# Attention score steps over two key tiles of one query chunk, with 64-row products for the queries' low parts

## The chip, the cores and the metric

One Trainium2 chip, one of its cores. The metric is device time in microseconds (us) of one launch; a kernel's time is the median of its runs. The engines are named as the profile names them: PE (TensorE matmuls), PEld (TensorE weight loads), DVE (VectorE), ACT (ScalarE), POOL (GpSimd), SP (SyncE, from whose queue all DMAs of this kernel are issued).

## The reference, cut to what matters

A squared-ReLU attention without softmax, gated by `u`, followed by a normalized gated feed-forward layer. All inputs are float32; 4 batches of 3008 tokens, width 256, query/key width 64, feed-forward width 1536.

```python
scores = scale * np.matmul(z, z.transpose(0, 2, 1))       # z: [4, 3008, 64], queries and keys are both z
attn = np.maximum(scores, 0.0) ** 2
out = np.matmul(attn, v)                                  # v: [4, 3008, 256]
x = (u * out).reshape(B * S, D)

rms = np.sqrt(np.mean(x * x, axis=-1, keepdims=True) + 1e-06)
xn = x / rms * rms_g
g = xn @ w_gate                                           # [256, 1536]
silu = g * (1.0 / (1.0 + np.exp(-g)))
val = xn @ w_val
y = silu * val @ w_out                                    # [1536, 256]
```

## The kernel before

**Precision.** Products run in a rounded float32 format (`F32R`). A float32 operand is split into a high part (a rounded copy) and a low part (what the copy left out), and a product of two operands becomes several matmuls that add up in one PSUM bank.

**Queries, keys.** `z` lies in memory twice, transposed: 128 rows, the 64 features and the same 64 again. For a chunk `c` of 512 keys, `prep_stat` makes the stationary tile `zst`: `one` (L278, on ACT) writes the high part of all 128 rows, `two` (L282, on DVE) overwrites rows 64 to 127 with the low part. So a key tile of 128 columns holds high parts above and low parts below. For the queries `prep_mov` makes `mh` and `ml`, high and low parts, each in both halves of the rows. A score tile (128 keys x 512 queries) is two matmuls into one `ps` bank: `zst` with `mh` (L366, 128 rows: high x high plus low x high) and `zst` with `ml` (L367, 128 rows: high x low plus low x low).

**Passes.** Work goes in 12 attention passes `phase_a(p)`, p = 0 to 11, three to a batch. A pass takes two neighbouring query chunks (`k` = 0, 1) and goes over the 24 key tiles of the batch in the order `order(p)`; step `i` takes key tile `i` for both chunks. In a step, `emit_s` makes the scores two steps ahead (`s_product` on PE, `s_relu` on ACT, `s_mult` on DVE: relu(s) times s), `emit_l` splits the squared scores one step ahead into `H` (a cast on ACT, L403) and `L` (a subtraction on DVE, L406; L410 for the last key tile), and `emit_av` multiplies them with the values: six matmuls for each chunk (L445, L446, L450) into four accumulators `po`. Four `ps` banks, six `r`, five `H` and five `L` buffers go round.

**Turned tiles.** Scores are symmetric, so some tiles are not computed twice: when a tile is first made, its squared scores go to memory (`halves`, a copy of 128x1024 16-bit words by ACT, L423, or DVE, L421, then a DMA to `kept`), and a later pass reads them back through a transposing DMA (`load_turned`, L345, one DMA for two key tiles of one chunk, into the ring `T` of six buffers). Of 576 score tiles in all, 392 are computed: 48, 48 and 44 in passes 0 to 2, then 44, 28 and 12 in each further batch. In passes 5, 8 and 11 most tiles are turned. Their loads are put at slot `i - 7` of the pass, for both chunks at even `i`.

**Feed-forward passes.** A feed-forward pass (`phase_m`, `Unit`, L644 to L676) for the pair of chunks three passes back follows each attention pass from pass 2 on. A list `pend` of closures carries the last value products of a pass, and `emit_gate` (L475, DVE: accumulator times `u`, then a DMA to `xg`), into what follows. `load_x` (L482) brings `xg` back as `ux`; `norm_jobs` squares, sums and scales it (L504 on ACT first). For p = 1, 4, 7, 10 these jobs run within attention pass p + 1: `load_x` is put at slot 9 there, the squares at slot 11.

**Order.** The order on each engine is the order of the code (a manual schedule). `at(phase, slot, fn)` puts a job into a slot, `hook` runs the slot's jobs in the order in which they were put there. Every engine, and SP's queue, runs its instructions in order, each waiting for what it needs.

Of the kernel before, what the change touches and what calls it, by code (L numbers as in the profile page):

```python
# [8 lines left out]
F32 = mybir.dt.float32  # L9
# [5 lines left out]
ALU = mybir.AluOpType  # L15
# [4 lines left out]
P = 128  # L20
CH = 512
# [9 lines left out]
def kernel(  # L31
# [13 lines left out]
    nc = tc.nc  # L45
    D, NT = uT.shape
    S = NT // batch
    DQK = zT2.shape[0] // 2
# [3 lines left out]
    NK = -(-S // P)  # L52
# [25 lines left out]
    def f32(ap):  # L78
        return ap.bitcast(F32)

    def where(p):

        b, j = divmod(p, NP)
        return b, 2 * j, b * S + j * PAIR, min(PAIR, S - j * PAIR)

    def width(c):
        return min(CH, S - c * CH)
# [10 lines left out]
    def at(phase, slot, fn):  # L98
        jobs[phase, slot].append(fn)
# [125 lines left out]
    zst = {}  # L225
    mov = {}
# [36 lines left out]
    def prep_stat(b, c, shared=None):  # L263
        t0 = c * CH
        n = width(c)
        m = n + TAIL if n < CH else n
        lo = slice(DQK, P)
        tiles = shared if shared is not None else {}

        def load():  # L270
            raw = tiles["raw"] = new_raw("batch" if b else "start")
            nc.sync.dma_start(out=raw[:, :n], in_=zT2[:, b * S + t0:b * S + t0 + n])
            if n < m:
                nc.sync.dma_start(out=raw[:, n:m], in_=zT2[:, (b + 1) * S - TAIL:(b + 1) * S])

        def one():
            z = zst[b, c] = keep.tile([P, CH], F32R, tag=f"zst{c}", name=f"zst{c}")
            nc.scalar.copy(z[:, :m], tiles["raw"][:, :m])  # L278

        def two():  # L280
            raw, z = tiles["raw"], zst[b, c]
            nc.vector.tensor_tensor(z[lo, :m], raw[lo, :m], f32(z[lo, :m]), op=ALU.subtract)  # L282

        return load, one, two

# [33 lines left out]
    att = {}  # L319
# [3 lines left out]
    def order(p):  # L323
        b, c0 = where(p)[:2]
        if p == 0:
            return list(range(NK))
        first = list(range(4 * (c0 + 1), min(4 * (c0 + 2), NK)))
        last = list(range(4 * c0, 4 * c0 + 4))
        return first + [k for k in range(NK) if k not in first and k not in last] + last
# [4 lines left out]
    def is_turned(p, i, k):  # L334
        b, c0 = where(p)[:2]
        kc = order(p)[i] // 4
        return kc < c0 + k and keeps(b, kc, c0 + k)
# [13 lines left out]

    scores = {}

    def s_product(p, i):
        b, c0 = where(p)[:2]
        kt = order(p)[i]
        for k in range(2):
            if is_turned(p, i, k):
                att[p, i, k] = turned.pop((p, i, k))
                continue  # L360
            n = width(c0 + k)
            mh, ml = mov[p, k]
            z = zst[b, kt // 4]
            ks = slice((kt % 4) * P, (kt % 4 + 1) * P)
            ps = ps_s.tile([P, CH], F32, tag="ps", name="ps")
            nc.tensor.matmul(ps[:, :n], z[:, ks], mh[:, :n], start=True, stop=False)  # L366
            nc.tensor.matmul(ps[:, :n], z[:, ks], ml[:, :n], start=False, stop=True)  # L367
            scores[p, i, k] = (n, ps)

    def s_relu(p, i, k):  # L370
        if (p, i, k) in scores:
            n, ps = scores[p, i, k]
            a = att[p, i, k] = work.tile([P, CH], F32, tag="r", name="r", bufs=6)
            nc.scalar.activation(a[:, :n], ps[:, :n], AF.Relu)  # L374

    def s_mult(p, i, k):
        if (p, i, k) in scores:
            n, ps = scores.pop((p, i, k))
            if not is_square(p, i, k):
                a = att[p, i, k]  # L380
                nc.vector.tensor_tensor(a[:, :n], ps[:, :n], a[:, :n], op=ALU.mult)  # L381

    def emit_s(p, i):
        s_product(p, i)
        for k in range(2):
            s_relu(p, i, k)
            s_mult(p, i, k)

    copies = [0]

    def emit_l(p, i, ks=(0, 1)):
        b, c0 = where(p)[:2]
        kt = order(p)[i]
        for k in ks:
            c = c0 + k
            n = width(c)
            a = att[p, i, k]
            hi = moving.tile([P, CH], F32R, tag="H", name="H", bufs=5)
            if is_square(p, i, k):
                nc.scalar.activation(hi[:, :n], a[:, :n], AF.Square)  # L400
                nc.scalar.activation(a[:, :n], a[:, :n], AF.Square)
            else:
                nc.scalar.copy(hi[:, :n], a[:, :n])  # L403
            if kt < NK - 1:
                lo = moving.tile([P, CH], F32R, tag="L", name="L", bufs=5)
                nc.vector.tensor_tensor(lo[:, :n], a[:, :n], f32(hi[:, :n]), op=ALU.subtract)  # L406
            else:
                lo = None
                h = slice(TAIL, P)
                nc.vector.tensor_tensor(hi[h, :n], a[h, :n], f32(hi[h, :n]), op=ALU.subtract)  # L410
            att[p, i, k] = (hi, lo)
            kc = kt // 4
            if kc > c and keeps(b, c, kc):
                if (b, kc, c) not in kept:
                    kept[b, kc, c] = dram.tile([2 * CH, CH], U16, tag=f"kept{kc}{c}", name=f"kept{kc}{c}")
                m = P if kt < NK - 1 else TAIL
                halves = work.tile([P, 2, CH], U16, tag="out", name="halves", bufs=3)
                split = a[:m].bitcast(U16).rearrange("p (q h) -> p h q", h=2)
                copies[0] += 1
                if c0 == 0 and copies[0] % 5 in (1, 3):  # L420
                    nc.vector.tensor_copy(halves[:m], split)  # L421
                else:
                    nc.scalar.copy(halves[:m], split)  # L423
                r0 = 2 * (kt % 4) * P
                nc.sync.dma_start(
                    out=kept[b, kc, c][r0:r0 + 2 * m, :].rearrange("(p h) q -> p h q", h=2), in_=halves[:m]
                )

    acc = {}

    def emit_av(p, i, k):
        b, c0 = where(p)[:2]
        n = width(c0 + k)
        kt = order(p)[i]
        if i == 0:
            for d in range(ND):
                acc[k, d] = ps_a.tile([P, CH], F32, tag=f"acc{k}{d}", name="po")
        po = [acc[k, d] for d in range(ND)]
        hi, lo = att.pop((p, i, k))
        wh, wl = vh[b, kt // 2], vl[b, kt // 2]  # L440
        j = kt % 2
        ends = i == NK - 1
        for d in range(ND):
            ds = slice(d * P, (d + 1) * P)
            nc.tensor.matmul(po[d][:, :n], wh[:, j, ds], hi[:, :n], start=(i == 0), stop=False)  # L445
            nc.tensor.matmul(po[d][:, :n], wl[:, j, ds], hi[:, :n], start=False, stop=(ends and lo is None))  # L446
        if lo is not None:
            for d in range(ND):
                ds = slice(d * P, (d + 1) * P)
                nc.tensor.matmul(po[d][:, :n], wh[:, j, ds], lo[:, :n], start=False, stop=ends)  # L450
# [317 lines left out]
    def phase_a(p):  # L768

        ph = ("A", p)  # L770
        for i in range(NK):
            if i + LA < NK:
                emit_s(p, i + LA)
            if i + 1 < NK:
                emit_l(p, i + 1)
            hook(ph, i)
            if i < NK - 2:
                emit_av(p, i, 0)
                emit_av(p, i, 1)
            elif i == NK - 2:  # L780
                emit_av(p, i, 0)

        def last(k):
            def go():
                emit_av(p, NK - 1, k)
                emit_gate(p, k)
            return go

        pend.extend([lambda: emit_av(p, NK - 2, 1), last(0), last(1)])

    def enter_a(p):
        return [lambda: emit_s(p, 0), lambda: (emit_s(p, 1), emit_l(p, 0))]
# [61 lines left out]
    for p in range(NPAIR):  # L854
        b, c0 = where(p)[:2]
        ph = ("A", p)
        m = beside[p] = Beside(p)

        for i in range(0, NK, 2):
            for k in range(2):  # L860
                if is_turned(p, i, k):
                    go = lambda p=p, i=i, k=k: load_turned(p, i, k)
                    if i < 8 and p >= LAG:
                        at(("M", p - LAG), 3 * (NF - 2 if i < 6 else NF - 1) + 1, go)
                    else:
                        at(ph, max(i - 7, 0), go)
        if p >= LAG - 1:
            for f in range(ahead(p - LAG + 1)):
                at(ph, NK - 3 + f, lambda p=p, f=f: load_unit(p - LAG + 1, f))
        at(ph, NK - 3, lambda p=p: load_u(p, [(0, 0)]))  # L870
        at(ph, NK - 1, lambda p=p: load_u(p, [(0, 1), (1, 0), (1, 1)]))
# [184 lines left out]
```

## Time and profile before

| | |
|---|---|
| median of 3 runs | 2098.78 us (2096.8 to 2103.1) |
| profiled execution | 2102.76 us, its span 2101.0 us |
| PE busy | 2041.3 us (97%), 8968 matmuls |
| PEld busy | 1687.7 us (80%) |
| DVE busy | 1618.2 us (77%) |
| ACT busy | 1426.3 us (68%) |
| POOL busy | 219.9 us (10%) |
| mean granted clock of PE | 0.989 |

A matmul's busy time runs from its start to its modelled end, and matmuls overlap; the distance of two starts says what one costs in a row of them. Times in the rows are us from the start of the span.

### The profile page before, as it was taken

The page shows a single profiled execution, that of the slowest core. Times are in us where ns is not written, and L with a number is a line of the kernel's source. Part 1 is how long each engine was busy: PE and PEld are TensorE (multiplying, and loading weights), DVE is VectorE, ACT ScalarE, POOL GpSimd, SP SyncE. Part 2 cuts the span into 40 slices and gives each one's busy share as a digit, 9 for nine tenths or more (in the row PEclk, how much of TensorE's full clock was granted, in tenths as well). Part 3 has the DMA queues.
Part 4 walks back from the last instruction along what each step waited for, and adds up shares of the span by engine and source line. Part 5 has one row for each costly group of instructions (what it writes and reads, how often), then busy time and mean ns, then how long its engine had stood idle before and what let it go on. Part 6 is the DMA issues. An engine that isn't in the chain of part 4 may idle for free.

```text
span 2101.0 us, 27215 instructions
## 1 busy us (share of the span) xinstructions
PE 2041.3 (97%) x8968; PEld 1687.7 (80%) x8968; DVE 1618.2 (77%) x2668; ACT 1426.3 (68%) x2566; POOL 219.9 (10%) x376
## 2 busy tenths in 40 slices
PE   8998989799999999999999999999999999999999
PEld 7776877688888878888887887888888788788887
DVE  8999987687777767787876776879777677577765
ACT  7776767596687565787577565679657757466665
POOL 0156752100000000400000000220000000000000
PEclk9999999899999999999999999999999999999999
DMA  3234474155456477526355548634544647634342
GB/s 107 89 118 149 127 228 163 68 185 190 121 141 200 137 169 211 171 99 219 133 151 153 175 134 193 222 112 159 196 136 131 202 135 159 172 132 162 123 143 89
DMA packets 320654, 320.50 MB, mean 153 GB/s; under 512 B 196736, under 2 KB 235776, under 8 KB 320512
## 3 DMA queue, kind: packets, MB, share of 16 engines
q1 hardware_dynamic: 320512, 318.77, 49.8%
q8 instruction: 70, 1.15, 0.2%
q14 instruction: 72, 0.59, 0.1%
HBM read 190.78 MB, written 81.79 MB: 130 GB/s over the span
## 4 chain that ended last, share of the span: by engine, by line
PE 81%; DVE 7%; issue 4%; ACT 3%; DMA 3%; POOL 1%; SPq 0%; DVEq 0%; ACTq 0%; POOLq 0%
PE po L445 11%; PE po L446 10%; PE po L450 10%; PE ps L644 10%; PE ps L645 9%; PE ps L646 9%; PE py L672 5%; PE py L673 5%; PE py L676 5%; PE ps L367 4%; PE ps L366 3%; DVE L L406 2%; DVE r L381 1%; POOL vl L313 1%; DMA ux<-xg 1%
## 5 line engine op out<-in xcount | busy, mean ns | idle before, releaser
L445 PE MATMUL po<-H,vh 128*128 128x512 f32 (+1 forms) x1152 | 452.1, 392 | 17.8 <-ACT H L403 10.5
L446 PE MATMUL po<-H,vl 128*128 128x512 f32 (+1 forms) x1152 | 448.3, 389 | 0.0
L644 PE MATMUL ps<-xh,wu 128*128 128x512 f32 (+1 forms) x1008 | 394.1, 391 | 15.0 <-DMA wu<-wc 12.0
L651 ACT COPY s<-ps 128x512 f32<-128x512 f32 (+1 forms) x432 | 249.5, 578 | 230.4 <-PE ps L646 230.4
L645 PE MATMUL ps<-xh,wu 128*128 128x512 f32 (+1 forms) x1008 | 390.9, 388 | 3.0 <-DMA wu<-wc 3.0
L646 PE MATMUL ps<-xl,wu 128*128 128x512 f32 (+1 forms) x1008 | 390.5, 387 | 0.0
L450 PE MATMUL po<-L,vh 128*128 128x512 f32 (+1 forms) x1104 | 339.7, 389 | 7.7 <-DVE L L406 7.6
L656 ACT CAST hH<-s 128x512 fp32r<-128x512 f32 (+1 forms) x288 | 176.6, 613 | 206.9 <-DVE s L738 203.8
L381 DVE TENSOR_TENSOR r<-ps,r 128x512 f32<-128x512 f32 (+1 forms) x363 | 235.5, 679 | 94.0 <-ACT r L374 93.1
L374 ACT ACTIVATE r<-ps 128x512 f32<-128x512 f32 (+1 forms) x392 | 216.4, 600 | 129.7 <-PE ps L367 115.4
L406 DVE TENSOR_TENSOR L<-r,H 128x512 fp32r<-128x512 f32 x368 | 256.6, 710 | 35.2 <-ACT H L403 32.1
L661 DVE TENSOR_TENSOR hL<-s,hH 128x512 fp32r<-128x512 f32 (+1 forms) x288 | 199.3, 692 | 104.8 <-ACT hH L656 91.6
L445 PEld LDWEIGHTS po<-H,vh 128*128 128x128 f32 x1152 | 219.0, 190 | 70.4 <-ACT H L403 13.1
L446 PEld LDWEIGHTS po<-H,vl 128*128 128x128 f32 x1152 | 219.0, 190 | 41.2
L450 PEld LDWEIGHTS po<-L,vh 128*128 128x128 f32 x1104 | 207.4, 189 | 51.8 <-DVE L L406 13.3
L644 PEld LDWEIGHTS ps<-xh,wu 128*128 128x128 f32 x1008 | 190.1, 189 | 61.7 <-DMA wu<-wc 12.9
L403 ACT CAST H<-r 128x512 fp32r<-128x512 f32 (+1 forms) x363 | 221.9, 631 | 5.1 <-DVE r L381 5.1
L672 PE MATMUL py<-hH,woh 128*128 128x512 f32 (+1 forms) x576 | 222.6, 386 | 0.1
L673 PE MATMUL py<-hH,wol 128*128 128x512 f32 (+1 forms) x576 | 222.3, 386 | 0.0
L645 PEld LDWEIGHTS ps<-xh,wu 128*128 128x128 f32 x1008 | 190.3, 189 | 38.6 <-DMA wu<-wc 3.8
L646 PEld LDWEIGHTS ps<-xl,wu 128*128 128x128 f32 x1008 | 190.3, 189 | 36.3
L313 POOL TENSOR_TENSOR vl<-raw,vh 128x128 fp32r<-128x128 f32 x144 | 75.5, 560 | 1022.7 <-ACT vh L302 1022.7
(82 smaller groups left out, 2876.0 us busy)
## 6 DMA issues: line engine op xcount, KB each, us to landing
wu<-wc SPq DMA_DIRECT2D x288, 448.0 KB, 4.0
kept<-halves SPq DMA_DIRECT2D x168, 256.0 KB, 2.0
raw<-in_v SPq DMA_DIRECT2D x44, 256.0 KB, 4.2
u<-in_uT SPq DMA_DIRECT2D x40, 256.0 KB, 4.2
xg<-u SPq DMA_DIRECT2D x40, 256.0 KB, 2.1
raw<-in_zT SPq DMA_DIRECT2D x38, 256.0 KB, 4.4
ux<-xg SPq DMA_DIRECT2D x16, 512.0 KB, 5.2
out_T<-y SPq DMA_DIRECT2D x32, 256.0 KB, 2.2
```

The lines of the kernel that those rows point to most:

```text
L381: nc.vector.tensor_tensor(a[:, :n], ps[:, :n], a[:, :n], op=ALU.mult)
L403: nc.scalar.copy(hi[:, :n], a[:, :n])
L406: nc.vector.tensor_tensor(lo[:, :n], a[:, :n], f32(hi[:, :n]), op=ALU.subtract)
L445: nc.tensor.matmul(po[d][:, :n], wh[:, j, ds], hi[:, :n], start=(i == 0), stop=False)
L446: nc.tensor.matmul(po[d][:, :n], wl[:, j, ds], hi[:, :n], start=False, stop=(ends and lo is None))
L450: nc.tensor.matmul(po[d][:, :n], wh[:, j, ds], lo[:, :n], start=False, stop=ends)
L644: nc.tensor.matmul(ps[:, :n], wh[:, o, :], xh[:, :n], start=start, stop=False, skip_group_check=True)
L645: nc.tensor.matmul(ps[:, :n], wl[:, o, :], xh[:, :n], start=False, stop=False, skip_group_check=True)
L646: nc.tensor.matmul(ps[:, :n], wh[:, o, :], xl[:, :n], start=False, stop=stop, skip_group_check=True)
L651: nc.scalar.copy(s, ps[:, :self.n])
L672: nc.tensor.matmul(acc[h, d][:, :n], woh[:, f, ds], hi[:, :n], start=(f == 0), stop=False)
L673: nc.tensor.matmul(acc[h, d][:, :n], wol[:, f, ds], hi[:, :n], start=False, stop=False)
```

## The change

A score step `s` now stands for one chunk and two key tiles: chunk `s % 2`, tiles `s - s % 2` and the next. `s_product` makes four matmuls: both tiles with `mh` on 128 rows, then both tiles with `ml`, each on 64 rows: the even tile's on rows 0 to 63, the odd tile's on rows 64 to 127. For that the high part must lie in those rows, so `two` now writes the low part into the lower rows of even key tiles and the upper rows of odd ones, in two instructions of 64x2x128. The product of low part and low part is no longer made. `emit_l`, `emit_av` and the pass's ends follow the new step, and the turned tiles of chunk 1 are loaded a slot later.

```diff
         def two():
             raw, z = tiles["raw"], zst[b, c]
-            nc.vector.tensor_tensor(z[lo, :m], raw[lo, :m], f32(z[lo, :m]), op=ALU.subtract)
+            for half in range(2):
+                rows = slice(DQK * (1 - half), DQK * (2 - half))
+                r, h = (t.rearrange("p (a b c) -> p a b c", b=2, c=P)[rows, :, half, :] for t in (raw, z))
+                nc.vector.tensor_tensor(h, r, f32(h), op=ALU.subtract)
...
-    def s_product(p, i):
+    def tiles_of(s):
+        return s % 2, (s - s % 2, s - s % 2 + 1)
+
+    def s_product(p, s):
         b, c0 = where(p)[:2]
-        kt = order(p)[i]
-        for k in range(2):
-            if is_turned(p, i, k):
+        k, pair = tiles_of(s)
+        if is_turned(p, pair[0], k):
+            for i in pair:
                 att[p, i, k] = turned.pop((p, i, k))
-                continue
-            n = width(c0 + k)
-            mh, ml = mov[p, k]
-            z = zst[b, kt // 4]
-            ks = slice((kt % 4) * P, (kt % 4 + 1) * P)
+            return
+        n = width(c0 + k)
+        mh, ml = mov[p, k]
+        for i in pair:
+            kt = order(p)[i]
             ps = ps_s.tile([P, CH], F32, tag="ps", name="ps")
-            nc.tensor.matmul(ps[:, :n], z[:, ks], mh[:, :n], start=True, stop=False)
-            nc.tensor.matmul(ps[:, :n], z[:, ks], ml[:, :n], start=False, stop=True)
-            scores[p, i, k] = (n, ps)
+            scores[p, i, k] = (n, ps, zst[b, kt // 4][:, (kt % 4) * P:(kt % 4 + 1) * P])
+            nc.tensor.matmul(ps[:, :n], scores[p, i, k][2], mh[:, :n], start=True, stop=False)
+        for i in pair:
+            n, ps, z = scores[p, i, k]
+            rows = slice(DQK * (i % 2), DQK * (i % 2 + 1))
+            nc.tensor.matmul(ps[:, :n], z[rows], ml[rows, :n], start=False, stop=True)
...
-        def last(k):
+        def last(s):
             def go():
-                emit_av(p, NK - 1, k)
-                emit_gate(p, k)
+                emit_av(p, s, 1)
+                emit_gate(p, s % 2)
             return go
 
-        pend.extend([lambda: emit_av(p, NK - 2, 1), last(0), last(1)])
+        pend.extend([last(NK - 2), lambda: emit_av(p, NK - 1, 0), last(NK - 1)])
...
-                        at(ph, max(i - 7, 0), go)
+                        at(ph, max(i + k - 7, 0), go)
```

On PE, at the start of the program (pass 0), the first rows of before are these; `ps` is a score tile, `zst` the keys, `po` the accumulators. The second score tile of a pair there is the other chunk's.

```order
L366 MATMUL ps<-mh,zst_97 128x512
L367 MATMUL ps<-ml,zst_97 128x512
L366 MATMUL ps<-mh,zst_97 128x512
L367 MATMUL ps<-ml,zst_97 128x512
L366 MATMUL ps<-mh,zst_97 128x512
L367 MATMUL ps<-ml,zst_97 128x512
```

The same place of the change (a row ending in x2 is two instructions; the shape is that of the output, so the 64 rows of the `ml` products don't show):

```order
L376 MATMUL ps<-mh,zst_97 128x512 x2
L380 MATMUL ps<-ml,zst_97 128x512 x2
L376 MATMUL ps<-mh,zst_97 128x512 x2
L380 MATMUL ps<-ml,zst_97 128x512 x2
L376 MATMUL ps<-mh,zst_97 128x512 x2
L380 MATMUL ps<-ml,zst_97 128x512 x2
L464 MATMUL po<-H,vh_105 128x512
L465 MATMUL po<-H,vl_107 128x512
```

The number of matmuls is the same, 392 of each kind; the two `ml` products of a step now follow each other directly, and so do the two `mh` products.

On SP's queue, in attention pass 5, around the two DMAs of `load_x` for pass 4 (`ux0`, `ux1`); `T` are the turned tiles, `kept4x` those of chunk 0, `kept5x` those of chunk 1. Before:

```order
L345 DMA_TRANSPOSE T_7764<-kept42_6263 128x2x1024
L345 DMA_TRANSPOSE T_7766<-kept52_6419 128x2x896
L345 DMA_TRANSPOSE T_7809<-kept43_6271 128x2x1024
L345 DMA_TRANSPOSE T_7811<-kept53_6427 128x2x896
L482 DMA ux0_7813<-xg4_6700 128x1024
L482 DMA ux1_7815<-xg4_6700 128x1024
L345 DMA_TRANSPOSE T_7857<-kept43_6271 128x2x1024
```

With the change:

```order
L348 DMA_TRANSPOSE T_7776<-kept42_6275 128x2x1024
L348 DMA_TRANSPOSE T_7799<-kept52_6431 128x2x896
L348 DMA_TRANSPOSE T_7821<-kept43_6314 128x2x1024
L501 DMA ux0_7823<-xg4_6699 128x1024
L501 DMA ux1_7825<-xg4_6699 128x1024
L348 DMA_TRANSPOSE T_7847<-kept53_6470 128x2x896
L348 DMA_TRANSPOSE T_7869<-kept43_6314 128x2x1024
```

The transposing load of chunk 1 that stood right ahead of the `ux` loads now stands behind them.

## Rows read from the trace of the kernel before

**Rows 1.** Page, part 4: the chain that ended last, by engine.

```profile
PE 81%; DVE 7%; issue 4%; ACT 3%; DMA 3%; POOL 1%; SPq 0%; DVEq 0%; ACTq 0%; POOLq 0%
```

**Rows 2.** Chain by line, in 11:98, 98:202, 202:303 and 404:494 us.

```profile
by line: PE po L445 19.5%; PE po L446 19.5%; PE po L450 18.8%; PE ps L367 10.4%; PE ps L366 9.9%; DVE L L406 4.8%; issue 2.3%; ACT H L403 2.2%; DVE r L381 2.0%; DVE ml L256 1.6%; DVE vl L308 1.5%; ACT r L401 1.5%; ACT r L374 1.4%; ACT H L40
by line: DVE L L406 13.8%; PE po L445 12.6%; PE po L446 12.0%; PE po L450 11.2%; DVE r L381 9.4%; issue 8.8%; PE ps L367 6.4%; PE ps L366 5.4%; DVE wt L152 1.9%; ACT r L374 1.9%; DVE ux L558 1.5%; ACT H L403 1.5%; DVE wraw L146 1.4%; DVE mi
by line: DVE L L406 12.7%; PE po L445 10.5%; DVE r L381 10.0%; PE po L446 9.8%; PE po L450 9.6%; issue 8.4%; DMA wu<-wc 6.6%; PE ps L645 3.6%; PE ps L366 3.5%; PE ps L367 3.5%; PE ps L646 3.3%; PE ps L644 2.8%; DVE xl L610 2.5%; DVE wraw L1
by line: PE po L445 24.0%; PE po L446 23.4%; PE po L450 22.7%; PE ps L366 10.1%; PE ps L367 10.1%; PE ps L645 2.8%; PE ps L646 2.8%; PE ps L644 2.8%; DVE y L684 0.8%; PE py L676 0.5%; PE py L673 0.3%; PE py L672 0.3%; issue 0.0%
```

**Rows 3.** Busy time by stretch: us, PE, PEld, DVE, ACT, POOL, PEclk, DMA, GB/s.

```profile
202.00:303.00 101.00, 94.00 (x401) 77.27 (x400) 93.85 (x144) 71.99 (x137) 69.58 (x108) 0.95 0.56 167
404.00:494.00 90.00, 89.94 (x396) 73.92 (x395) 74.77 (x122) 76.67 (x130) 0.00 (x0) 1.00 0.55 188
```

**Rows 4.** Timeline of PE, a score step of pass 0: start, us, what.

```profile
43.46 0.39 PE L366 MATMUL ps<-mh,zst 128*128 128x512 f32 x1
...
44.37 0.39 PE L445 MATMUL po<-H,vh 128*128 128x512 f32 x1
...
47.09 0.39 PE L366 MATMUL ps<-mh,zst 128*128 128x512 f32 x1
```

**Rows 5.** Chain in order of time, pass 5: start, us, what.

```profile
774.88 0.64 DVE L L406
775.52 1.38 SPq L345
...
776.95 0.58 SPq L482
...
777.58 5.96 DMA ux<-xg
```

**Rows 6.** Timeline of PE, passes 5, 8 and 11; in brackets idle before, releaser.

```profile
784.75 0.80 PE L445 MATMUL po<-H,vh 128*128 128x512 f32 x1 [3.66 <-ACT H L403]
...
1289.99 0.50 PE L445 MATMUL po<-H,vh 128*128 128x512 f32 x1 [3.09 <-ACT H L403]
...
1796.12 0.50 PE L445 MATMUL po<-H,vh 128*128 128x512 f32 x1 [3.79 <-ACT H L403]
```

**Rows 7.** Busy time by stretch, just after two of those waits.

```profile
783.50:790.40 6.90, 5.65 (x14) 4.77 (x15) 4.98 (x9) 5.21 (x10) 0.00 (x0) 0.51 0.58 116
...
1797.40:1800.70 3.30, 3.30 (x10) 2.83 (x9) 2.34 (x5) 1.67 (x4) 0.00 (x0) 0.50 0.81 155
```

**Rows 8.** Groups by line and form: busy us, mean ns, idle before.

```profile
L367 PEld LDWEIGHTS ps<-ml,zst 128*128 128x128 f32 x392 | 75.1, 192 | 17.2 <-DVE ml L256 2.6
...
L381 DVE TENSOR_TENSOR r<-ps,r 128x512 f32<-128x512 f32 x336 | 220.8, 685 | 93.5 <-ACT r L374 92.7
...
L381 DVE TENSOR_TENSOR r<-ps,r 128x448 f32<-128x448 f32 x27 | 16.6, 613 | 0.5 <-ACT r L374 0.5
...
L282 DVE TENSOR_TENSOR zst<-raw,zst 64x512 fp32r<-64x512 f32 x24 | 16.6, 690 | 0.8
```

**Rows 9.** Timeline of PE around the two 32-column matmuls of L522.

```profile
800.65 0.39 PE L367 MATMUL ps<-ml,zst 128*128 128x512 f32 x1
800.88 0.30 PE L522 MATMUL ps<-misc,fold_sb 128*128 128x32 f32 x2
801.02 0.48 PE L445 MATMUL po<-H,vh 128*128 128x512 f32 x1
```

**Rows 10.** Timeline of ACT, pass 4: casts one step apart.

```profile
635.41 0.70 ACT L403 CAST H<-r 128x512 fp32r<-128x512 f32 x1
...
639.30 0.72 ACT L403 CAST H<-r 128x512 fp32r<-128x512 f32 x1
```

**Rows 11.** Timeline of DVE, pass 5, the second subtraction of a step.

```profile
772.29 0.63 DVE L406 TENSOR_TENSOR L<-T,H 128x448 fp32r<-128x448 f32 x1 [0.58 <-ACT H L403]
```

**Rows 12.** Timeline of DVE, first feed-forward unit after pass 5.

```profile
819.67 0.69 DVE L734 TENSOR_TENSOR s<-s 128x512 f32<-128x512 f32 x1 [2.51 <-ACT s L651]
```

More of the change, by code (lines that the diff above doesn't have):

```diff
@@ L266, in prep_stat @@
         m = n + TAIL if n < CH else n
-        lo = slice(DQK, P)
+        assert m == CH
         tiles = shared if shared is not None else {}
@@ L352, with s_relu, s_mult @@
     scores = {}
-    def s_product(p, i):
+    def tiles_of(s):
+        return s % 2, (s - s % 2, s - s % 2 + 1)
+    def s_product(p, s):
         b, c0 = where(p)[:2]
-        kt = order(p)[i]
-        for k in range(2):
-            if is_turned(p, i, k):
+        k, pair = tiles_of(s)
+        if is_turned(p, pair[0], k):
+            for i in pair:
                 att[p, i, k] = turned.pop((p, i, k))
-                continue
-            n = width(c0 + k)
-            mh, ml = mov[p, k]
-            z = zst[b, kt // 4]
-            ks = slice((kt % 4) * P, (kt % 4 + 1) * P)
-            ps = ps_s.tile([P, CH], F32, tag="ps", name="ps")
-            nc.tensor.matmul(ps[:, :n], z[:, ks], mh[:, :n], start=True, stop=False)
-            nc.tensor.matmul(ps[:, :n], z[:, ks], ml[:, :n], start=False, stop=True)
-            scores[p, i, k] = (n, ps)
-    def s_relu(p, i, k):
-        if (p, i, k) in scores:
[L372 to L378, printed above, removed]
+            return
[3 more added lines that the diff above has]
+            kt = order(p)[i]
+            ps = ps_s.tile([P, CH], F32, tag="ps", name="ps")
+            scores[p, i, k] = (n, ps, zst[b, kt // 4][:, (kt % 4) * P:(kt % 4 + 1) * P])
[4 more added lines that the diff above has]
+            nc.tensor.matmul(ps[:, :n], z[rows], ml[rows, :n], start=False, stop=True)
+    def s_relu(p, s, j):
+        k, pair = tiles_of(s)
+        if (p, pair[j], k) in scores:
+            n, ps, _ = scores[p, pair[j], k]
+            a = att[p, pair[j], k] = work.tile([P, CH], F32, tag="r", name="r", bufs=6)
+            nc.scalar.activation(a[:, :n], ps[:, :n], AF.Relu)
+    def s_mult(p, s, j):
+        k, pair = tiles_of(s)
+        i = pair[j]
+        if (p, i, k) in scores:
+            n, ps, _ = scores.pop((p, i, k))
             if not is_square(p, i, k):
@@ L381, in s_mult, with emit_s, emit_l @@
                 nc.vector.tensor_tensor(a[:, :n], ps[:, :n], a[:, :n], op=ALU.mult)
[L383 to L387, printed above, removed]
+    def emit_s(p, s):
+        s_product(p, s)
+        for j in range(2):
+            s_relu(p, s, j)
+            s_mult(p, s, j)
     copies = [0]
-    def emit_l(p, i, ks=(0, 1)):
+    def emit_l(p, s, js=(0, 1)):
         b, c0 = where(p)[:2]
[L393 to L396, printed above, removed]
+        k, pair = tiles_of(s)
+        c = c0 + k
+        n = width(c)
+        for j in js:
+            i = pair[j]
+            kt = order(p)[i]
             a = att[p, i, k]
@@ L429, with emit_av @@
     acc = {}
-    def emit_av(p, i, k):
+    def emit_av(p, s, t):
         b, c0 = where(p)[:2]
+        k, pair = tiles_of(s)
+        i = pair[t]
         n = width(c0 + k)
```

## The prediction, made before the change was run

> **What bounds the kernel now.** I read first the chain that ended last: 81% of it is PE, DVE 7% [rows 1]. So a matmul taken off PE is worth what it costs there, in each stretch in which the chain really runs through the score products. That is the second view, the chain by line in four stretches [rows 2]. The score products L366 and L367 hold 20.3% of it in pass 0 (11 to 98 us), 11.8% from 98 to 202, 7.0% from 202 to 303, and 20.2% in pass 3 (404 to 494). In passes 1 and 2 the DVE lines L406 and L381 take over much of the chain. The busy times say the same [rows 3]: from 202 to 303 DVE is busy 93.85 of 101 us, in pass 3 DVE and ACT 74.77 and 76.67 of 90, where PE is full.
>
> What a score product costs is seen in a step of pass 0 [rows 4]: from the first L366 to the first L445 are four matmuls, 44.37 - 43.46 = 0.91 us or 227 ns each, although each is drawn as 390 ns long; a whole step is 47.09 - 43.46 = 3.63 us, sixteen times 227 ns, so PE has no gap there.
>
> A second thing bounds passes 5, 8 and 11. The chain leaves PE there [rows 5]: a subtraction of DVE ends at 775.52 and frees a buffer of the ring `T`, the last transposing load (SP, L345) then takes 1.38 us more on the queue, only then come the two `ux` loads, and the data land 5.96 us after the second one's issue, at 783.54. ACT's squares stand ahead of its casts and wait for that, and PE waits for a cast: 3.66, 3.09 and 3.79 us in the three passes [rows 6]. After the first and the third of these waits the granted clock stood at 0.51 and 0.50, the 1.2 GHz level, for 6.9 and 3.3 us [rows 7]; what PE did before was to stand idle.
>
> **The change, part by part.**
>
> *The low products.* 392 score tiles are computed [rows 8], so there are 196 pairs. The number of matmuls stays; what can change is that the two `ml` products of a pair use different rows of the array, different rows of memory and different PSUM banks, so that the second need not wait until the first one's 512 columns are through. No matmul in this trace uses fewer than 128 rows, so I bound it. Below: nothing, the second starts 227 ns after the first [rows 4]. Above: both at once, 227 ns saved for each pair. The nearest row is L522 [rows 9], where what follows need not wait for 512 columns: its two 32-column matmuls and their weight loads take 801.02 - 800.88 = 0.14 us from start to start of what follows, 70 ns for a load with its matmul. I take that: the second low product starts 70 ns after the first, and the pair saves 227 - 70 = 157 ns.
>
> The Trainium skill, "TensorE: Matmul & The Clock Gate", Part 3, says that matmuls on different row groups run concurrently, started about 4 ns apart. No run here shows it; by that figure the saving would be an estimated 223 ns for each pair, near the upper bound.
>
> Against it stands the change of row count: 128 to 64 and back, twice in each step. Below it costs nothing: each matmul in rows 4 starts while the one before is drawn as running, and the passage from 512 to 32 columns and back in rows 9 costs nothing that shows. Above, PE waits for the modelled end of the last matmul, 390 - 227 = 163 ns each time. I take 20 ns each, near the lower end, since the nearest change of shape (rows 9) shows none. Net saving of a pair: 157 - 40 = 117 ns.
>
> *How many pairs count.* The score products' time on the chain divided by 0.91 us for a pair's four matmuls: 20.3% of 87 us is 17.7 us or 19.5 pairs; 11.8% of 104 is 12.3 us or 13.5; 7.0% of 101 is 7.1 us or 7.8. In passes 3, 6 and 9 all of it is on the chain (20.2% of 90 us is 18.2 us for the 20 pairs there): 3 x 22 = 66. In passes 4, 7 and 10 there are 14 pairs each, but the eight steps that also write turned copies are paced by ACT: its casts come 639.30 - 635.41 = 3.89 us a step [rows 10], more than PE's 3.63. So 6 each, 18. Passes 5, 8 and 11 have 6 each, 18. Together 143 pairs, and 143 x 0.117 = 16.7 us.
>
> *The order on SP's queue.* In passes 5, 8 and 11 chunk 1's transposing load moves from slot 9 to slot 10, behind the `ux` loads. The one that stays ahead (chunk 0) needs the buffer whose two tiles are now both split one step earlier, where before chunk 1's split of that step ended: 772.29 + 0.63 = 772.92 [rows 11]. With 1.38 us for the load the first `ux` issue comes at 774.30 in place of 776.95 [rows 5]: 2.65 us earlier. All of it comes off PE's waits, since each is longer [rows 6]: 3 x 2.65 = 7.9 us. The stretches at half clock lost 3.4 and 1.7 us [rows 7]; with waits of about 1 us left I count 3 of these 5.1 as gained. The load that moved now has a step less to land, but chunk 1's tiles are also taken a step later, so nothing new waits.
>
> *The split of the keys.* Twice 24 instructions of 256 elements for 24 of 512, 690 ns each. From the two forms of L381, 685 and 613 ns for 512 and 448 elements [rows 8], one of 256 would take 685 - 4 x 72 = 397, a pair 794: 104 ns more. Six lie in pass 0, 0.6 us at most; the others lie in feed-forward passes, where DVE waits [rows 12].
>
> *The gate of chunk 0* moves up by one entry of `pend`. It may now wait on DVE for its `u`, and L734 stands behind it; DVE idles 2.51 us ahead of L734 already, for ACT [rows 12], so I cost it at nothing (without that cover, its two instructions, some 1.3 us in each pass).
>
> *Sum.* -16.7 - 7.9 - 3 + 0.6 = -27.0 us. The profiled execution took 2102.76 us (span 2101.0), 4 us over the median of 2098.78; the sum is a difference within it, and I apply it to the median: 2098.8 - 27.0, about 2072 us. The span should be some 2074.
>
> **Rivals.**
>
> *The change of row count drains PE* (slower). Each of the two changes waits for the modelled end, 163 ns: a pair then costs 326 - 157 = 169 ns more, 143 x 0.169 = 24.2 us; the queue's 7.9 us still comes off, 0.6 is added, the clock gives nothing back: 2098.8 + 16.9, about 2116. For it: every row of PE shows that 163 ns between next start and modelled end, and nothing shows that the overlap survives such a change. Against it: 32-column matmuls slip in without a wait. It decides from 115 ns a change upward, where 143 x (2 x 0.115 - 0.157) = 10.4 us eats the other gains. The Trainium skill, "TensorEngine Tiling (Array Packing)", Key Properties, states just this, that changing the tiling mode drains the engine; no run here shows it.
>
> *No overlap.* The two low products follow each other at 227 ns, and nothing is saved on PE; the queue's part alone gives 2098.8 - 10.3 = 2088. For it: no row shows two matmuls side by side. Against it: the rows of array, memory and PSUM that they use are disjoint.
>
> *DVE and ACT become the bound.* Half of the pairs' gain is lost because DVE (93% busy in rows 3) and ACT (85% in pass 3) can't follow a shorter step: 2072 + 8, 2080. For it: rows 3 and 10. Against it: a step of pass 3 would shrink by 0.12 of 3.63 us only.
>
> **How the numbers follow.** About 0.3% (6.3 us) is what a measurement of this kernel can tell from no change: 2092.5 to 2105.1 counts as the same. Chances: my forecast 0.52 (own range 2054 to 2086), the drain in whole or part 0.26 (2095 to 2116 and beyond; 0.07 of it within the same), no overlap 0.13 (0.08 faster, 0.05 same), DVE and ACT 0.06 (faster), anything else 0.03, slower and same alike. Faster 0.66, same 0.13, slower 0.21. Range: the best case is 227 ns on 143 pairs, 32.5 us, with 7.9 and 5.1, which is 2053; upward it goes through most of the drain case, to 2110, and leaves out the full drain and what lies beyond.
>
> **What would show it.** In the profile after: the second L380 of a pair starts some 70 ns after the first (drain or not), or 227 (no overlap); the first L380 starts 0.23 to 0.25 us after the second L376 (forecast) or 0.39 (drain), and the first L464 some 0.25 or 0.39 after the second L380; a full step of pass 0 takes 3.51 us in place of 3.63; PE's longest wait in passes 5, 8 and 11 is about 1 us, and the clock stays at the upper level there. I would be wrong if the changes of row count show as gaps on PE, if weight loads for 64 rows can't go ahead of the running matmul, or if the waits of PE for `H` and `L` grow by what the matmuls give back.

## The result, and the profile after

The change made the kernel slower by 0.7%: 2116.0 us (median of 5 runs, 2112.6 to 2118.9) against 2102.8 (median of 5 runs in all, 2096.8 to 2104.3); ratio 1.0071, 95% interval 1.0051 to 1.0091. The forecast was 2072 and faster. The profiled execution took 2118.89 us; its page gives the span and each engine's busy time, share and instructions.

```profile
span 2117.1 us, 27247 instructions
PE 2070.4 (98%) x8968; PEld 1634.6 (77%) x8968; DVE 1624.5 (77%) x2692; ACT 1428.6 (67%) x2566; POOL 220.4 (10%) x376
```

PE runs as many matmuls as before and is busy 29 us longer. Where, a step of pass 0 shows, in the timeline of PE after (start, us, what; a row with x2 is two instructions). It answers to [rows 4].

```profile
61.18 0.61 PE L376 MATMUL ps<-mh,zst 128*128 128x512 f32 x2
61.73 0.50 PE L380 MATMUL ps<-ml,zst 64*128 64x512 f32 x2
62.16 0.50 PE L464 MATMUL po<-H,vh 128*128 128x512 f32 x1
62.50 0.40 PE L465 MATMUL po<-H,vl 128*128 128x512 f32 x1
62.73 0.39 PE L464 MATMUL po<-H,vh 128*128 128x512 f32 x1
...
65.01 0.39 PE L376 MATMUL ps<-mh,zst 128*128 128x512 f32 x1
```

The step takes 65.01 - 61.18 = 3.83 us, before 3.63. The two L380 share one row of 0.50 us: they run side by side (in the trace their starts lie 3 ns apart, median of all pairs of 512 columns). What they gave is lost around them, at the two places where the row count changes. The medians over the steps, against 227 ns everywhere before: second L376 to first L380 318 ns; first L380 to first L464 430, where two products one behind the other would take 454; first L464 to L465 338. In the 430 ns, as the runs below show, the second part of the change to 64 rows and the first part of the change back are paid out of what the overlap gains. So these three distances are 91 + 111 - 24 = 178 ns longer together than before; the whole step is longer by 0.20 us.

The weight loads of the same place (PEld; in brackets idle time before, and its releaser) show why.

```profile
60.96 0.41 PEld L376 LDWEIGHTS ps<-mh,zst 128*128 128x128 f32 x2
61.73 0.19 PEld L380 LDWEIGHTS ps<-ml,zst 64*128 64x128 f32 x2 [0.35 <-issue]
62.16 0.19 PEld L464 LDWEIGHTS po<-H,vh 128*128 128x128 f32 x1 [0.24 <-issue]
62.27 0.19 PEld L465 LDWEIGHTS po<-H,vl 128*128 128x128 f32 x1
```

L376's first load starts 0.22 us ahead of its matmul, beside the matmul then running. L380's and L464's start with their own matmul (61.73, 62.16), after 0.35 and 0.24 us in which nothing that the profile shows held them. These are the two places where the row count changes. The groups by line and form say it for the whole kernel (busy us, mean ns of one, idle before and its releasers): an L380 is drawn 504 ns long, an L376 397, and nearly all of the 69.4 us of idle time ahead of L380's loads is "issue". The last row is the keys' split.

```profile
L376 PE MATMUL ps<-mh,zst 128*128 128x512 f32 x360 | 113.5, 397 | 10.8 <-DVE mh L255 5.6 <-DVE zst L285 5.2
L380 PE MATMUL ps<-ml,zst 64*128 64x512 f32 x360 | 91.3, 504 | 0.0
L380 PEld LDWEIGHTS ps<-ml,zst 64*128 64x128 f32 x392 | 36.9, 185 | 69.4 <-issue 67.3 <-DVE ml L256 1.1 <-DVE zst L285 0.7
L285 DVE TENSOR_TENSOR zst<-raw,zst 64x256 fp32r<-64x256 f32 x48 | 20.2, 420 | 1.1
```

PE's long waits in passes 5, 8 and 11 answer to [rows 6]; they shrank by 0.85, 0.67 and 1.38 us.

```profile
793.12 0.74 PE L464 MATMUL po<-H,vh 128*128 128x448 f32 x1 [2.81 <-ACT H L420]
1304.26 0.74 PE L464 MATMUL po<-H,vh 128*128 128x448 f32 x1 [2.42 <-ACT H L420]
1814.18 0.47 PE L464 MATMUL po<-H,vh 128*128 128x448 f32 x1 [2.41 <-ACT H L420]
```

The stretches behind them answer to [rows 7] (the column ahead of the last two is PEclk): the clock still falls to the 1.2 GHz level for a time behind two of the three waits, those of passes 5 and 8; before, it was 5 and 11.

```profile
793.00:800.00 7.00, 6.88 (x19) 5.92 (x20) 5.85 (x11) 4.70 (x10) 0.00 (x0) 0.56 1.02 205
1304.00:1311.00 7.00, 6.74 (x24) 5.89 (x25) 5.85 (x11) 5.05 (x11) 0.00 (x0) 0.76 1.03 210
1814.00:1821.00 7.00, 6.82 (x32) 5.99 (x33) 5.84 (x11) 5.37 (x12) 0.00 (x0) 1.00 0.97 206
```

The passes, each from its first to its last value product with `vh` and `H` (L445 before, L464 after), in us, summed over passes of one kind; the columns on the right are runs told below:

| passes | before | change | all rows | loads of ux earlier, alone | old slots | all rows, ux earlier |
|---|---|---|---|---|---|---|
| 0 | 87.16 | 92.25 | 86.16 | 86.90 | 92.73 | 86.29 |
| 1, 2 | 199.76 | 199.38 | 198.18 | 197.74 | 201.39 | 198.77 |
| 3, 6, 9 | 265.74 | 277.67 | 266.69 | 265.30 | 277.56 | 266.45 |
| 4, 7, 10 | 248.93 | 251.35 | 249.40 | 246.51 | 251.33 | 249.40 |
| 5, 8, 11 | 232.97 | 228.30 | 223.38 | 217.90 | 235.35 | 216.76 |

Before to change: passes 0, 3, 6 and 9, full of computed tiles, lose 17.0 us; 5, 8 and 11 gain 4.7; the sum over all passes is +14.4.

### The profile page after: what moved, and what is told of

The parts are those of the page before. It is cut to its first block, busy times and chain, and to the rows that moved or that the text cites. A ratio compares the mean times of both kernels' runs of the same rounds, so it can differ in the third digit from the quotient of the medians.

```text
span 2117.1 us, 27247 instructions
## 1 busy us (share of the span) xinstructions
PE 2070.4 (98%) x8968; PEld 1634.6 (77%) x8968; DVE 1624.5 (77%) x2692; ACT 1428.6 (67%) x2566; POOL 220.4 (10%) x376
## 5 line engine op out<-in xcount | busy, mean ns | idle before, releaser
L464 PE MATMUL po<-H,vh 128*128 128x512 f32 (+1 forms) x1152 | 470.3, 408 | 9.4 <-ACT H L420 7.6
L465 PE MATMUL po<-H,vl 128*128 128x512 f32 (+1 forms) x1152 | 449.1, 390 | 0.0
L464 PEld LDWEIGHTS po<-H,vh 128*128 128x128 f32 x1152 | 218.4, 190 | 94.7 <-issue 34.6
L423 DVE TENSOR_TENSOR L<-r,H 128x512 fp32r<-128x512 f32 (+1 forms) x368 | 255.1, 711 | 39.3 <-ACT H L420 35.4
L465 PEld LDWEIGHTS po<-H,vl 128*128 128x128 f32 x1152 | 219.1, 190 | 35.5
```

## The experiments

Theory A: each change of the row count, 128 to 64 or back, costs PE some 200 ns, and two of them outweigh the 224 ns that a pair gains side by side. Theory B: the new order of steps, its waits or its queue order, made the kernel slower. A ratio is always to the kernel before, run on the same chip.

**Low products on all 128 rows**, the rest of the change kept.

```diff
-            nc.tensor.matmul(ps[:, :n], z[rows], ml[rows, :n], start=False, stop=True)
+            nc.tensor.matmul(ps[:, :n], z, ml[:, :n], start=False, stop=True)
```

> The change with its low products on all 128 rows; its order of steps, its key layout and its queue order stay. Theory A (each change of row count costs PE some 200 ns: about 91 ns until the array is free and about 108 ns of weight load that no longer runs beside the matmul before; two changes in a step, and 224 ns come back because the pair runs at once): no change of row count is left, a full step of pass 0 takes 3.63 us again, the second-to-third matmul of a step starts 227 ns after the one before, time 2097 to 2104 us, about that of the kernel before. Theory B (the new order of the step, two tiles of one chunk with both high products first, makes ACT and DVE late): the step stays near 3.83 us, time about 2116.

Measured: 2089.3 us, ratio 0.9944 [0.9927, 0.9961], faster than before and below what either theory expected. PE's timeline of a step:

```profile
42.39 0.62 PE L376 MATMUL ps<-mh,zst 128*128 128x512 f32 x2
42.85 0.61 PE L380 MATMUL ps<-ml,zst 128*128 128x512 f32 x2
43.30 0.39 PE L464 MATMUL po<-H,vh 128*128 128x512 f32 x1
```

Four matmuls again take 0.91 us. B falls: the new order alone gains 11.3 us, and the 64 rows cost 2116.0 - 2089.3 = 26.7 us. Most of the gain lies in passes 5, 8 and 11 (232.97 to 223.38), where the waits in brackets are 1.25, 2.55 and 1.74 us; part of it is the clock (below, under the queue and the clock).

**Both low products on rows 0 to 63**: the changes of row count stay, the overlap goes. The keys are split as before.

```diff
-            rows = slice(DQK * (i % 2), DQK * (i % 2 + 1))
+            rows = slice(0, DQK)
```

> The change with both low products of a step on rows 0 to 63 (keys split as before), so that they can't run at once. Theory A: two changes of row count a step as in the change, but 224 ns more for the pair; a full step of pass 0 takes 3.63 + 0.40 = 4.03 us, and with 143 pairs on the path 143 x 0.40 = 57 us: about 2155 us. Theory B: the overlap has nothing to do with it, time near 2116.

Measured: 2156.5 us (its profiled execution 2148.5), ratio 1.0253 [1.0233, 1.0272]. PE's timeline:

```profile
61.40 0.61 PE L374 MATMUL ps<-mh,zst 128*128 128x512 f32 x2
61.95 0.73 PE L378 MATMUL ps<-ml,zst 64*128 64x512 f32 x2
62.61 0.50 PE L462 MATMUL po<-H,vh 128*128 128x512 f32 x1
62.94 0.40 PE L463 MATMUL po<-H,vl 128*128 128x512 f32 x1
...
65.46 0.61 PE L374 MATMUL ps<-mh,zst 128*128 128x512 f32 x2
```

That is near A's 2155. With nothing side by side the price stands bare. The medians are 318, 335, 323 and 337 ns from the second high product to the second value product, in place of 227 each. So each change costs about 91 to 96 ns before the first matmul of the new row count starts and 108 to 110 ns before the second: some 200 ns, and by the whole step, 4.05 against 3.63, 0.43 us for the two. Side by side saves 4.05 - 3.83 = 0.22 us of the step.

**The order of before, each low product on rows 0 to 63**: four changes in a step.

```diff
-            nc.tensor.matmul(ps[:, :n], z[:, ks], ml[:, :n], start=False, stop=True)
+            nc.tensor.matmul(ps[:, :n], z[:DQK, ks], ml[:DQK, :n], start=False, stop=True)
```

> The kernel before with each low product on rows 0 to 63 alone (the product of low part and low part is left out, as in the change), in the old order high, low, high, low: four changes of row count in a step, and no two matmuls side by side. Theory A (each change costs PE about 200 ns): a full step of pass 0 takes 3.63 + 0.80 = 4.43 us and the time is 2100 + 143 x 0.80, about 2215 us, less where DVE covers it. Rival (what costs is the pair on two halves, or the new order, not the change of row count): as the kernel before, 2100.

Measured: 2229.7 us, ratio 1.0611 [1.0587, 1.0635]. PE's timeline, a step from 62.49 to 66.91:

```profile
62.49 0.39 PE L366 MATMUL ps<-mh,zst 128*128 128x512 f32 x1
62.80 0.50 PE L367 MATMUL ps<-ml,zst 64*128 64x512 f32 x1
63.23 0.49 PE L366 MATMUL ps<-mh,zst 128*128 128x512 f32 x1
63.66 0.50 PE L367 MATMUL ps<-ml,zst 64*128 64x512 f32 x1
64.09 0.50 PE L445 MATMUL po<-H,vh 128*128 128x512 f32 x1
...
66.91 0.39 PE L366 MATMUL ps<-mh,zst 128*128 128x512 f32 x1
```

The step is 4.43 us, 0.80 over 3.63: 0.20 for each of four changes, in an order of steps that knows nothing of the pairs. The time is 15 us above A's 2215.

**High products on 64 rows too**, side by side like the low ones.

```diff
-            nc.tensor.matmul(ps[:, :n], scores[p, i, k][2], mh[:, :n], start=True, stop=False)
+            rows = slice(DQK * (i % 2), DQK * (i % 2 + 1))
+            nc.tensor.matmul(ps[:, :n], scores[p, i, k][2][rows], mh[rows, :n], start=True, stop=False)
```

> The change with its high products on 64 rows too, each tile on its own half, so that a step has four 64-row matmuls in two pairs (the keys' low part times the queries' high part is left out). Theory A1 (only the change of row count stops weight loads from running ahead; between 64-row pairs they run ahead): two changes a step as in the change, but one more pair side by side: a full step of pass 0 takes 3.83 - 0.22 = 3.61 us, time about 2116 - 143 x 0.22 = 2084 us. Theory A2 (a 64-row matmul never gets its weights ahead): the second pair costs some 110 to 200 ns more, step 3.72 to 3.81, time 2100 to 2113.

Measured: 2090.1 us, ratio 0.9946 [0.9927, 0.9966]. PE's timeline:

```profile
61.51 0.50 PE L377 MATMUL ps<-mh,zst 64*128 64x512 f32 x2
61.84 0.40 PE L381 MATMUL ps<-ml,zst 64*128 64x512 f32 x2
62.17 0.50 PE L465 MATMUL po<-H,vh 128*128 128x512 f32 x1
```

and the weight load of its second pair (PEld):

```profile
61.61 0.19 PEld L381 LDWEIGHTS ps<-ml,zst 64*128 64x128 f32 x2
```

The first pair behind the change is drawn 0.50 us long, the second 0.40, which is the usual length: from 64 rows to 64 rows the load runs ahead again, 0.23 us before its own products (61.61 and 61.84). The price belongs to the change, not to 64-row matmuls. Two pairs side by side for two changes come out 14 ns ahead of before (step 3.613). The time is 6 us above A1's and level with all rows (2089.3): what this version gains over before is the order's gain of the first run, not the pairs'.

**Two pairs of low products behind four high ones** (`e4_quad`; the eight products are a quad): two changes for two steps.

```diff
+        for k in range(2):
+            for i in tiles_of(s + k)[1]:
+                if (p, i, k) in scores:
...
+                    nc.tensor.matmul(ps[:, :n], z[rows], mov[p, k][1][rows, :n], start=False, stop=True)
```

> The change with the score products of two steps made together: four high products, then the two pairs of low products, so two changes of row count for four tiles in place of two. Theory A: 0.40 us of changes against 2 x 0.224 saved for four tiles, 48 ns less than the kernel before for each four; two full steps of pass 0 take 7.21 us (7.26 before, 7.66 with the change); time 2092 to 2100. Theory B: the high products come still further ahead of the low ones and four PSUM banks are asked for at once, so no faster than 2116.

Measured: 2106.5 us, ratio 1.0026 [1.0015, 1.0037]. Two steps take 7.24 us (change 7.66, before 7.25): two changes cost nearly what two pairs gain, and 14 ns are left where A had 48. But the time missed its forecast by some 10 us. I took the entry of each pass, where four high products now stand ahead, to be the cause, and made the first two steps of a pass single again (`e7_quad_entry`):

> The quads of e4_quad, but a pass's first two steps made singly, so that its entry asks for two PSUM banks at once and not four. If e4_quad fell short of its forecast because the entry waits for the banks of the feed-forward unit: the 1.6 us that it loses between the passes (88.45 against 86.83 us after pass 3) shrink to the 0.5 us of the change, nine times, 2094 to 2099 us. If the quads themselves cost it: 2106 again.

Measured: 2104.3 us, ratio 1.0016 [1.0007, 1.0026]: 2 us less, and the stretch after pass 3 has not shrunk (88.68 us). I had misread it: it holds 386 matmuls, before 382, so 0.9 of the 1.6 us are four score products that moved there out of the pass. The first quad of a pass is late still. That of pass 4 takes 2.07 us to the first value product at 585.50, a later one 1.66:

```profile
583.43 1.48 PE L379 MATMUL ps<-mh,zst 128*128 128x512 f32 x4
```

In pass 3 it takes 2.66, with PE held for 0.36 us by DVE's product, which reads a `ps` bank: so four banks asked for at once do cost something, as theory B has it. In pass 4 PE also waits 0.36, 0.48 and 0.54 us for `H` where the computed tiles end (with the change once, 0.44). These parts make up most of the 1 us or so that is lost in a pass; no run takes them away one by one. With the loads of `ux` a slot earlier as well (below; PE's waits with quads are 2.4 to 2.9 us by the trace, not 2.7 to 3.2):

> e7_quad_entry with the ux loads one slot earlier, as in e3_loadx8. The waits of passes 5, 8 and 11 go as there (they are still 2.7 to 3.2 us in e4_quad): 5 to 10 us less than e7_quad_entry, 2085 to 2092, so not better than e3_loadx8 (2084) by more than 1 us.

Measured: 2097.9 us, ratio 0.9984 [0.9975, 0.9994]: 6.4 us off, but 6 us above the forecast.

**The kernel before with the loads of `ux` one slot earlier** (`e3_loadx8`), a version without any of the change.

```diff
-            at(("A", p + 1), 9, lambda p=p: load_x(p))
+            at(("A", p + 1), 8, lambda p=p: load_x(p))
```

> The kernel before with the ux loads one slot earlier in the attention passes, ahead of both transposing loads of slot 9. If the waits of PE in passes 5, 8 and 11 are set by the place of the ux loads in SP's queue, where each transposing load takes some 2.1 us whatever it waits for: the loads go out about 4 us earlier, the waits of 3.66, 3.09 and 3.79 us go to under 0.5, the clock stays at the upper level there, 10 to 15 us less: 2088 to 2093. If they are set by a buffer or by ACT's order: no more than 3 us less.

Measured: 2084.3 us, ratio 0.9917 [0.9902, 0.9932]. That is 4 us below the forecast. PE's waits in passes 5, 8 and 11 are gone (the only idle time over half a us is one of 0.58 late in pass 5), and these passes are 15.1 us shorter in sum. Why the queue was late shows on SP (start, us, what), before:

```profile
753.52 3.88 SPq L345 DMA_TRANSPOSE T<-kept  x2
757.50 0.55 SPq L425 DMA_DIRECT2D kept<-halves  x1
759.72 17.18 SPq L345 DMA_TRANSPOSE T<-kept  x8
776.95 1.06 SPq L482 DMA_DIRECT2D ux<-xg  x2
```

and in the change:

```profile
764.10 21.93 SPq L348 DMA_TRANSPOSE T<-kept  x9
786.08 1.05 SPq L501 DMA_DIRECT2D ux<-xg  x2
```

A transposing load passes SP in (3.88 + 17.18) / 10 = 2.1 us before and 21.93 / 9 = 2.4 after, on average, and from 759.72 on one behind the other without a gap. The loads of `ux` wait for this procession. Two loads fewer ahead of them are worth 4.4 us of their time, which is more than the wait of [rows 6]. Two loads held by a buffer would have been passed in the same way, so this run alone does not tell the two causes apart. A load of pass 4 of the kernel before does: it stands alone between other DMAs, no wait of it ends in that time, and it takes as long:

```profile
625.75 2.60 SPq L345 DMA_TRANSPOSE T<-kept  x1
```

**The change with chunk 1's turned loads back in the old slots.**

```diff
-                        at(ph, max(i + k - 7, 0), go)
+                        at(ph, max(i - 7, 0), go)
```

> The change, with chunk 1's turned loads back in the slots of before, so that in passes 5, 8 and 11 ten transposing loads pass SP's queue ahead of the loads of ux, not nine. Theory A (the change of row count costs PE some 200 ns each time; the queue order gave back a little): the waits of PE in passes 5, 8 and 11 grow from 2.4 to 2.8 us to some 4 to 5 us each, and the time is 5 to 9 us above the change, 2121 to 2125. Theory B (the queue order gave nothing or did harm): 2116 or below. Steps of pass 0 stay at 3.83 us by both.

Measured: 2129.2 us, ratio 1.0134 [1.0113, 1.0154], 13 us above the change (11.4 by the profiled spans): the direction of A, by more than expected. PE's waits:

```profile
799.40 0.74 PE L464 MATMUL po<-H,vh 128*128 128x448 f32 x1 [4.69 <-ACT H L420]
...
1314.07 0.74 PE L464 MATMUL po<-H,vh 128*128 128x448 f32 x1 [6.79 <-ACT H L420]
...
1825.48 0.47 PE L464 MATMUL po<-H,vh 128*128 128x448 f32 x1 [3.27 <-ACT H L420]
```

SP in passes 5 and 8:

```profile
768.49 22.27 SPq L348 DMA_TRANSPOSE T<-kept  x10
790.82 1.04 SPq L501 DMA_DIRECT2D ux<-xg  x2
...
1281.08 24.63 SPq L348 DMA_TRANSPOSE T<-kept  x10
1305.76 1.05 SPq L501 DMA_DIRECT2D ux<-xg  x2
```

The tenth load alone adds some 2.4 us; in pass 8 the ten also pass slower. Of the 11.4 us, 7.1 lie in these passes; 2.0 lie in passes 1 and 2, and 1.9 in the stretch behind pass 2, where the granted clock was 0.61 from 308.3 to 313.0 us (with the change 1.00 there), which I had not counted. So the later slot for chunk 1 is what the order gains: this version is 28.9 us above before, and the 64 rows cost 26.7 of them. All rows with the old slots, which would show it directly, was not run.

**All rows and the loads of `ux` a slot earlier**: the first run's edit and the slot of 8.

> The change with its low products on all 128 rows (so no change of row count), and the loads of ux one slot earlier. By theory A nothing on PE is left to pay, and the two gains of the queue overlap: the waits in passes 5, 8 and 11 go below 0.5 us, those passes shorten from 73.3, 76.3 and 73.8 us to about 72.6, some 6 us less than with all rows alone: 2082 to 2085, level with the kernel before with the loads of ux one slot earlier (2084). If the paired order has a gain of its own beside the queue's, 2075 to 2080.

Measured: 2082.8 us, ratio 0.9916 [0.9901, 0.9931], as A says; no different from the one slot alone (0.9917). SP in pass 5, and the one wait of PE that is left in passes 5, 8 and 11:

```profile
750.98 18.16 SPq L348 DMA_TRANSPOSE T<-kept  x8
769.20 1.04 SPq L501 DMA_DIRECT2D ux<-xg  x2
```

```profile
778.04 0.47 PE L464 MATMUL po<-H,vh 128*128 128x448 f32 x1 [0.84 <-ACT H L420]
```

The order by pairs has nothing of its own beside the queue's gain. No version here is clearly faster than the kernel before with one number changed.

## Why the prediction was wrong, step by step

**The step that failed** is the price of the change of row count: "I take 20 ns each, near the lower end, since the nearest change of shape (rows 9) shows none." It is some 200 ns. [rows 9] were no near row: there the columns change, 512 to 32, but both matmuls stand on 128 rows. The upper bound, 163 ns, was too low as well: it was made of the wait for the running matmul alone. What the rows show is two parts, 91 to 96 ns before the first matmul of the new row count, and 105 to 111 ns before the one behind it, where the weight load no longer runs ahead. That the second part is the load is a reading of the rows: the load starts with its own matmul (61.73, 62.16), that matmul is drawn 504 ns long in place of 397, and both go away between two 64-row pairs. What the first part is made of no run shows. The text had named both under what would make it wrong, gaps on PE and weight loads that can't go ahead, and had priced only the first.

**The second low product** starts 3 ns after the first, not 70: 67 ns too careful for each pair. The overlap, on which the forecast most depended, is there in full.

**The sum mended.** With 143 pairs, 200 in place of 20 ns adds 143 x 2 x 0.180 = 51.5 us, and 3 in place of 70 takes off 9.6: -27.0 + 51.5 - 9.6 = +14.9. Measured +13.2 (2116.0 - 2102.8). With 213 ns, half of the 426 that the step gives for two changes, it would be +18.6, so the closeness is in part luck.

**The count of pairs** holds in the sum, less so in its parts. By the step a pair loses 203 ns, and 143 of them 29.0 us; the run with all rows puts the 64 rows at 26.7 by the medians and 29.1 by the profiled spans (2117.1 - 2088.0). By the table (change less all rows) it is 6.1 us in pass 0, 1.2 in 1 and 2, 11.0 in 3, 6 and 9, 2.0 in 4, 7 and 10, and 4.9 in 5, 8 and 11, with 3.6 between the passes. The counts would give 4.0, 4.3, 13.4, 3.7 and 3.7: the parts are off by up to 3 us and make up for each other. The runs with both low products on the same rows and with four changes put 55.8 / 0.426 = 131 and 128.8 / 0.80 = 161 pairs on the path.

**The queue and the clock** have about the right sum for another reason, which is luck. Forecast were 7.9 and 3 us, less 0.6 for the keys; the run with all rows gains 11.3. But `ux` does not come 2.65 us earlier: counted from the first value product of the pass it is issued 0.17 us earlier in pass 5 (786.08 - 755.71 against 776.95 - 746.41). The prediction took the link in the chain, DVE to SP [rows 5], for what held the queue; from 759.72 on the queue was full of loads without a gap. One load less ahead is worth 2.1 us, but the procession starts 1.28 us later after the pass's start (764.10 - 755.71 against 753.52 - 746.41) and takes 2.4 us a load. The waits shrank by 2.9 us in all, not 7.9, and the half clock stayed behind two of them. With all rows the waits shrink by 5.0, and passes 5, 8 and 11 gain 9.6. Pass 8 has no share in this (75.92 to 76.29 us), and the clock shows why. Its wait is only 0.54 us shorter, and the half clock, which stood behind the waits of passes 5 and 11 before, stands behind that of pass 8 with all rows, and there alone (1.00 in the other two); 0.76 over 7 us loses 1.7. Before, then with all rows:

```profile
1290.00:1296.90 6.90, 6.90 (x32) 5.92 (x32) 5.69 (x11) 5.27 (x11) 0.00 (x0) 1.00 0.69 143
```

```profile
1282.00:1289.00 7.00, 6.75 (x24) 5.73 (x25) 5.85 (x11) 5.03 (x11) 0.00 (x0) 0.76 1.02 202
```

**The keys' split** costs 2 x 420 - 690 = 150 ns a chunk, forecast 104; six in pass 0, 0.9 us at most.

**The rivals.** The drain had the time, 2116, by luck, with parts that were off in opposite ways: 163 ns a change was 37 too low, twice a pair, and 70 for the second start 67 too high. The first L380 starts at 61.73; the second L376 started at 61.41 (61.18 + 0.23) and would end, at 390 ns, at 61.80, so PE does not wait for the modelled end. Whether it waits for the real one can't be seen, since the ends are modelled. The Trainium skill, "TensorEngine Tiling (Array Packing)", Key Properties, says that a change of tiling mode drains the engine; the trace agrees that it costs, some 200 ns each time. No overlap falls by the 3 ns (its 2088 had also left out 5.7 us, the prediction's own 20 ns a change). DVE and ACT as the bound did not come to a trial, since the steps became longer.

**What stays open**: what the 91 to 96 ns ahead of a changed row count are made of, the parts of the 1 us or so a pass in the kernels with quads, and why a transposing load holds SP's queue now 1.5 us, now 3.5.

## What to carry to other kernels

Side-by-side 64-row products gain one product's time, 224 ns at 512 columns; to go over to them and back costs 400 to 430 ns. So they pay only if at least two such pairs stand together between the two changes, and then hardly; collect more, or leave the rows whole. A bound for an unseen price should be taken from a row in which the same thing changes, and should include the load that is no longer hidden. And where a chain names a buffer as what held a queue, look first whether the queue stood idle at all, and how long one entry takes where it waits for nothing.

## What the runs showed of the hardware that was not expected

Two products on rows 0 to 63 and 64 to 127 start 3 ns apart; the Trainium skill, "TensorE: Matmul & The Clock Gate", Part 3, gives about 4 ns, and the trace agrees.

The same part says in a list that a weight load overlaps a running matmul only when it is for other rows; a sentence above that list also allows a load into the background weight buffer. The trace differs from the list: a load for 128 rows starts 0.22 us ahead of its matmul beside another 128-row matmul (60.96 and 61.18), and 64-row loads run ahead between two pairs; it is where the row count changes that the load comes late (61.73, 62.16).

A transposing load of two tiles holds SP's queue for 2.1 to 2.5 us on average (1.45 to 3.56 for a single one in pass 5 before and with the change), and ten of them in a row for 21 to 25 us; what stands behind them waits that long.
